# Whole-block stores and head-by-head loads for 18-wide heads, last tokens between projections, paired contraction tails, and new segment orders

## The chip, the cores and the metric

One core of one Trainium2 chip. The metric is device time in microseconds (us), the median of several executions.

Words used throughout: a **segment** is one of 64 turns of a recurrence; a **step** is one unit of ordinary attention (scores of four heads, one exp over 128 x 2048, weighing) that is threaded into the segments. The **loop** is the 64 segments, the **prologue** what comes before the first projection of segment 0, the **end** the last segment and the finish. In the views, a line gives start and length in us, engine, line of the kernel and operation; brackets give the idle time before it and what ended it; `SPq` is a DMA issued by SyncE. `pvv` are the projections of `A`, `psh`, `pss` and `pso` its scores, row sums and weighing, `acc` its output projection, `tm` a copied projection on its way to memory or to `v_sb` (the values). `sb`, `etb` and `ob` are scores, exp and weighing of `B`.

## The reference

```python
g = sigmoid((x * gate_w).sum(-1, keepdims=True))
return g * A(x, mem0, Wq, Wk, Wv, Wo) + (1 - g) * B(B_x, wqkv, wo)

def A(...):                     # x 2048 x 576, 32 heads of 128, 8 memory tokens, segments of 32
    mem = mem0
    for s in range(64):
        h = concatenate([mem, x[32*s:32*s+32]])         # 40 tokens
        q, k, v = h @ Wq, h @ Wk, h @ Wv                # 576 -> 32 x 128 each
        p = softmax(where(mask, q @ k.T * 128**-0.5, -1e9))
        o = (p @ v) @ Wo
        mem, out_s = o[:8], o[8:]                       # the next segment needs mem

def B(...):                     # plain attention, 2048 tokens, 32 heads of 18 = 576/32
    q, k, v = split(B_x @ wqkv); return softmax(q @ k.T * 18**-0.5) @ v @ wo
```

All arrays are bfloat16. `A` is a chain of 64 segments. `B` is 512 steps, and the kernel fills the chain's waits with them.

## The kernel before

A segment's 40 tokens are treated as 32 plus the last 8. The last 8 do not depend on the memory, so their projections are done ahead, for 16 segments at a time ("last tokens"), stored in memory and loaded again. The inner dimension of 576 is four blocks of 128 and a tail of 64 rows; the tail's weights lie in one tile, two halves above each other, and each projection multiplied the tail against all 128 rows, half of them zeros.

```python
def project(x, w, b, k):                     # one of six per segment: Q0 Q1 K0 K1 V0 V1
    pv = bank(k, [P, 512], FP32, "pvv")
    for c in range(NF + 1):                  # four blocks and the tail
        for j in range(4):                   # four column tiles side by side
            rw, cc = w_slice(w, c, ..., 512)
            nc.tensor.matmul(pv[32*j:32*j+32, :], lhsT=ht[:, cc, :], rhs=rw,
                             start=(c == 0), stop=(c == NF), tile_position=(0, 32*j))

def store_v(x, b):                           # V goes to v_sb by four stores for each of V0, V1
    for jj in range(2):
        for u in range(2):
            nc.sync.dma_start(out=v_sb[64*jj:64*jj+CT, ...], in_=sbt[x][64*jj+32*u: ..., :])

def load_kv(g, kc):                          # B's keys, four heads padded to 32 rows each
    kch[g, kc] = bint.tile([P, KC * P], BF16, name="kch", bufs=6)
    loads.dma_start(out=kch[g, kc][:, :], in_=ktd[g, :, kc * KC * P:(kc + 1) * KC * P])
    ...
```

The order in which a segment's instructions are issued is written out by hand as a string. `B` and `E` are the two halves of a step, `Q0` is a projection, `cQ0` its copy out of PSUM, `v0` the four stores of V0, `S0` scores, `x0` exp, `n0` the causal minimum, `p0` row sums, `l0` and `r0` logarithm and inverse, `m0` the division, `w00` weighing, `o00` its copy, `a00` the output projection, `F0` a filler (last tokens of later segments, or output rows). There is one string for segments with seven steps and one for those with eight:

```python
        8: """
        Q0 B E : V0 cQ0 K0 cV0 v0 B / cK0 E : tq0 pq0 Q1 tk0 pk0 cQ1 B / E : S0 K1 tq1 x0 cK1 B n0 tk1 E
        : V1 pk1 pq1 p0 cV1 v1 S1 l0 r0 x1 / B E : F0 m0 n1 w00 o00 F1 cF0 p1 w01 o01 cF1 l1 r1 m1 B F2
        a00 cF2 w10 o10 w11 E : B E : o11 ol a01 a10 h0 a11 g0 B h1 g1 f0 E : f1 ht0 ht1 oh og
        """.split(),
...
LOAD_LAST = "r1"          # where in the last segment the loads for the finish are issued
```

(`:` and `/` let small leftovers of `A` and `B` run.) The number of eight-step segments is whatever is left of the 512 steps: the steps that the prologue has not done. The last-token fillers run out after segment 46; the output rows go on, in two of every four segments.

The softmax here doesn't subtract the row's maximum and nothing guards it: scores larger than these inputs give would overflow.

## Time and profile before

1617.18 us, median of 3 runs (1617.07 to 1620.35); the profiled execution spans 1613.9 us at a mean clock of 0.986. All stage figures are read the same way: the start of the first matmul of the first projection in each segment, in TensorE's timeline.

| stage (profiled run) | before, us |
|---|---|
| prologue | 174.55 |
| segment 0 | 23.02 |
| segments 1 to 22, mean (seven steps) | 21.88 |
| segments 23 to 46, mean | 22.25 |
| segments 47 to 62, mean (eight steps, no last-token fillers) | 21.58 |
| last segment and finish | 55.64 |

First the page's row of the granted clock, in tenths of full speed for 40 slices of the span:

```profile
PEclk9899999999999999999999999999999999999999
```

Then the windows by stage: length, busy time and count of each engine, then the mean granted clock, the DMA share and GB/s. The first line is segments 47 to 62, the second the end:

```profile
1212.97:1558.28 345.31, 315.00 (x5744) 160.33 (x5742) 210.18 (x537) 274.46 (x225) 55.50 (x130) 1.00 0.17 35
1558.28:1613.90 55.62, 44.06 (x571) 28.07 (x571) 33.43 (x77) 31.61 (x46) 11.97 (x23) 0.96 0.49 150
```

And on SyncE's timeline the eight stores of V in one eight-step segment (1320.95 to 1343.00):

```profile
1324.72 11.59 SPq L772 DMA_DIRECT2D v_sb<-tm  x8
```

### The profile page before, as it was taken

The numbers are of one execution on the slowest core, as the hardware profiler recorded it, in microseconds if no ns is written. First come the engines' busy times: TensorE is split into PE (matmuls) and PEld (weight loads), VectorE is DVE, ScalarE is ACT, GpSimd is POOL, SyncE is SP. The second block draws the span as 40 slices with busy tenths as digits, with TensorE's granted clock in tenths as the row PEclk, the third lists the DMA queues.
The fourth block names the chain that finished last, engine by engine and source line by source line (L and its number), as shares of the span: only waits on it lengthen the run. The fifth ranks groups of instructions, "written<-read, shape, count | busy, mean of one in ns | idle before, by whom it ended". The sixth has DMA issues, their size and how long they took to land.

```text
span 1613.9 us, 57766 instructions
## 1 busy us (share of the span) xinstructions
PE 1476.7 (91%) x25082; PEld 782.0 (48%) x25082; DVE 960.0 (59%) x2355; ACT 1139.8 (71%) x981; POOL 338.4 (21%) x731
## 2 busy tenths in 40 slices
PE   6598899999999999999999999999999989998997
PEld 3434444555454444555454445555554444444445
DVE  2233666666566666666566666666666656565656
ACT  2165577777677767777677777777777777788774
POOL 6311211213131031302121211212121212120131
PEclk9899999999999999999999999999999999999999
DMA  7788322212122121212122121212221121211125
GB/s 200 235 291 290 100 65 64 49 42 52 45 50 53 32 53 38 61 36 49 43 43 60 38 50 40 57 39 45 51 53 35 30 48 34 45 34 35 29 59 162
DMA packets 209865, 114.39 MB, mean 71 GB/s; under 512 B 159491, under 2 KB 197251, under 8 KB 208019
## 3 DMA queue, kind: packets, MB, share of 16 engines
q1 hardware_dynamic: 188971, 58.40, 16.1%
q0 software_dynamic: 19696, 50.02, 9.9%
q8 instruction: 196, 3.21, 0.9%
q10 hardware_dynamic: 944, 2.29, 0.4%
q14 instruction: 58, 0.48, 0.1%
HBM read 60.94 MB, written 36.10 MB: 60 GB/s over the span
## 4 chain that ended last, share of the span: by engine, by line
PE 69%; ACT 11%; DVE 11%; DMA 4%; issue 2%; SPq 1%; POOL 1%; DVEq 0%; ACTq 0%; POOLq 0%
PE pvv L755 27%; ACT etb L257 9%; PE sb L238 8%; PE ob L222 7%; PE pt L782 5%; PE pv L326 4%; PE psh L800 3%; PE acc L643 3%; PE pso L838 3%; PE pv L313 2%; DVE hl L657 2%; PE pq L420 2%; DVE hl L654 2%; DVE ot L850 2%; ACT rq L830 2%
## 5 line engine op out<-in xcount | busy, mean ns | idle before, releaser
L257 ACT ACTIVATE etb<-sb 128x2048 bf16<-128x2048 f32 x512 | 959.6, 1874 | 341.9 <-PE sb L238 341.1
L767 DVE CAST tm<-pvv 128x512 bf16<-128x512 f32 x384 | 264.4, 689 | 175.1 <-PE pvv L755 174.2
L755 PEld LDWEIGHTS <-ht 128*32 128x32 bf16 x7680 | 185.8, 97 | 183.7 <-DVE ht L891 14.1
L238 PE MATMUL sb<-qch,kch 32*128 32x512 bf16 x2048 | 203.2, 386 | 38.5 <-ACT etb L257 36.7
L222 PE MATMUL ob<-etb,vch 128*32 128x512 bf16 x2048 | 205.9, 392 | 3.9 <-DVE tq L159 3.9
L850 DVE CAST ot<-pso 128x320 bf16<-128x320 f32 x256 | 120.7, 488 | 104.2 <-PE pso L838 99.9
L643 PE MATMUL acc<-wo,ot 128*32 128x384 bf16 (+1 forms) x4096 | 159.7, 291 | 5.4 <-DVE ot L850 3.3
L755 PE MATMUL pvv<-wq_m,ht 128*32 128x512 bf16 x2048 | 134.2, 382 | 13.0 <-DVE ht L891 8.3
L755 PE MATMUL pvv<-wk_m,ht 128*32 128x512 bf16 x2048 | 134.9, 384 | 0.0
L755 PE MATMUL pvv<-wv_m,ht 128*32 128x512 bf16 x2048 | 134.3, 382 | 0.0
L643 PEld LDWEIGHTS <-ot 128*32 128x32 bf16 x4096 | 105.2, 98 | 46.5 <-DVE ot L850 12.8
L700 POOL DMA_DIRECT2D a_dram<-rl x186 | 92.6, 506 | 162.4 <-DVE rl L695 143.3
L238 PEld LDWEIGHTS <-kch 32*128 32x128 bf16 x2048 | 61.2, 91 | 128.5 <-issue 107.9
L857 POOL COPY otl<-ot 128x256 bf16<-128x256 bf16 x64 | 25.9, 405 | 445.6 <-DVE ot L850 445.6
L222 PEld LDWEIGHTS <-vch 128*32 128x32 bf16 x2048 | 52.9, 93 | 120.6 <-issue 116.0
L782 PE MATMUL pt<-ident,tm 128*128 128x128 bf16 x1024 | 96.8, 221 | 0.8 <-DVE tm L767 0.8
L790 DVE COPY kt<-pt 128x512 bf16<-128x512 bf16 x128 | 54.0, 422 | 69.4 <-PE pt L782 69.0
L838 PE MATMUL pso<-et,v_sb 64*128 64x40 bf16 x2048 | 81.4, 178 | 14.9 <-DVE hll L657 4.7
L838 PEld LDWEIGHTS <-v_sb 64*128 64x128 bf16 x2048 | 62.8, 93 | 62.4 <-issue 49.5
L654 DVE CAST hl<-acc 128x384 bf16<-128x384 f32 (+1 forms) x128 | 57.9, 452 | 58.1 <-PE acc L643 57.8
L782 PEld LDWEIGHTS <-tm 128*128 128x128 bf16 x1024 | 57.8, 98 | 67.0 <-issue 49.4
L826 ACT ACTIVATE lt<-pss 128x320 f32<-128x320 f32 x128 | 56.0, 438 | 43.2 <-PE pss L822 32.8
(141 smaller groups left out, 1847.4 us busy)
## 6 DMA issues: line engine op xcount, KB each, us to landing
v_sb<-tm SPq DMA_DIRECT2D x512, 32.0 KB
wo<-in_A_Wo_dram POOLq DMA_DIRECT2D x4, 1152.0 KB, 9.7
wv_m<-in_A_Wv_dram POOLq DMA_DIRECT2D x4, 1024.0 KB, 8.0
wq_m<-in_A_Wq_dram POOLq DMA_DIRECT2D x4, 1024.0 KB, 9.1
wk_m<-in_A_Wk_dram POOLq DMA_DIRECT2D x4, 1024.0 KB, 8.0
xl<-qld SPq DMA_DIRECT2D x64, 64.0 KB
xl<-kld SPq DMA_DIRECT2D x64, 64.0 KB
v_sb<-vld SPq DMA_DIRECT2D x128, 32.0 KB
```

Of the source, the lines that this page charges most:

```text
L222: nc.tensor.matmul(ob[32 * j:32 * j + 32, :], lhsT=vc[:, o + 32 * j:o + 32 * j + 32], rhs=et4[:, j, :], start=(kb == 0), stop=(kb == NKB - 1),
L238: nc.tensor.matmul(sb[:, j, :], lhsT=kc[32 * j:32 * j + 32, o:o + P], rhs=qch[gq][32 * j:32 * j + 32, :], start=True, stop=True, tile_posi ...
L257: nc.scalar.activation(out=before[:, :, :], in_=sb[:, :, :], func=ACT.Exp, scale=scale_b)
L326: nc.tensor.matmul(pv[:, o:o + P], lhsT=lw, rhs=xlb[:, cc, :], start=(c == 0), stop=(c == NF))
L643: nc.tensor.matmul(acc[32 * j:32 * j + 32, 0:d1 - d0], lhsT=o[:, h, 0:CT], rhs=wo[:, h, d0:d1], start=(b == 0 and i == 0), stop=(b == 1 an ...
L654: nc.vector.tensor_copy(out=hl[:, 0, d0:d1], in_=acc[:, 0:d1 - d0])
L700: eng.dma_start(out=rows4[m, seg - LO:seg, i * n:(i + 1) * n], in_=rl[32 * i + m * LO:32 * i + (m + 1) * LO, :],)
L755: nc.tensor.matmul(pv[32 * j:32 * j + 32, :], lhsT=ht[:, cc, :], rhs=rw, start=(c == 0), stop=(c == NF), tile_position=(0, 32 * j),)
L767: nc.vector.tensor_copy(out=sbt[x][:, :], in_=ps[x][:, :])
L782: nc.tensor.transpose(out=pt[:, which, :, :, :].rearrange("p j (u i) t -> p j u i t", i=4)[:, :, :, i, :], in_=sbt[x][:, i * Dh:(i + 1) * Dh],
L838: nc.tensor.matmul(pso[:, i * L:(i + 1) * L], lhsT=v_sb[64 * jj:64 * jj + 64, b * 1024 + i * Dh:b * 1024 + (i + 1) * Dh], rhs=et[64 * jj:6 ...
L850: nc.vector.tensor_copy(out=ot[:, j * HG:(j + 1) * HG, :].rearrange("p h t -> p (h t)"), in_=ps["o", b, jj][:, 0:W8],)
```

## The change

Four intentions. **Queries and keys of B** are stored in whole 128-row blocks; the padding to 32 rows a head happens at the load, by head, into tiles zeroed once, so nine stores cut at the heads' edges and all pad stores go. **Last tokens** are threaded between the projections of the prologue. **Tails are paired**: two projections' 64-row tails use the upper and the lower half of the array at once. **New orders** for both kinds of segment, as the pairs ask for, made with the projections near the front. The final loads move with the order (`LOAD_LAST`).

```diff
-    qtd = dpool.tile([GB, P, S], BF16, name="qtd")
-    ktd = dpool.tile([GB, P, S], BF16, name="ktd")
+    qkd = dpool.tile([2 * Dm, S], BF16, name="qkd")
...
+        def load_heads(eng, t, f, t0):
+            for j in range(4):
+                eng.dma_start(
+                    out=t[32 * j:32 * j + DhB, :], in_=qkd[f + j * DhB:f + (j + 1) * DhB, t0:t0 + QC]
+                )
...
+    def store_qk(blk):
+        nc.sync.dma_start(out=qkd[blk * P:(blk + 1) * P, :], in_=stgs[blk][:, :])
...
+        for _ in range(2 * min(t, 1)):       # value weights fetched early
+            next(pieces)
...
+    for i, blk in enumerate((1, 6, 2, 7, 3, 8)):
         for t in range(NQC):
             project_qk(blk, t, 0)
             between(1.1)
-        store_qk(blk, range(GB))
+            if i > 0:
+                some_tokens()                # two halves of a last-token block
+        store_qk(blk)
...
+        def project_tails(two):
+            two = [(x, w, b, begin(x)) for x, w, b in two]
+            for j in range(4):
+                for x, w, b, first in two:
+                    t, r = w_tail(w, columns(b, j), 512)
+                    nc.tensor.matmul(
+                        ps[x][32 * j:32 * j + 32, :],
+                        lhsT=ht[TL * r:TL * r + TL, NF + r, :],
+                        rhs=t[TL * r:TL * r + TL, :],
+                        start=first, stop=(not first),
+                        tile_position=(TL * r, 32 * j), skip_group_check=True,
+                    )
...
         8: """
-        Q0 B E : V0 cQ0 K0 cV0 v0 B / cK0 E : tq0 pq0 Q1 tk0 pk0 cQ1 B / E : S0 K1 tq1 x0 cK1 B n0 tk1 E
-        : V1 pk1 pq1 p0 cV1 v1 S1 l0 r0 x1 / B E : F0 m0 n1 w00 o00 F1 cF0 p1 w01 o01 cF1 l1 r1 m1 B F2
-        a00 cF2 w10 o10 w11 E : B E : o11 ol a01 a10 h0 a11 g0 B h1 g1 f0 E : f1 ht0 ht1 oh og
+        Q0 B T0 cQ0 K0 T1 E : cK0 B K1 E : Q1 cQ1 B cK1 V0 T2 E : tk0 tq0 pk0 B E : pq0 / V1 S0 cV0 v0
+        tq1 B cV1 v1 tk1 pq1 x0 F1 n0 pk1 E : p0 / S1 / cF1 x1 n1 l0 F2 F0 p1 r0 l1 r1 m0 cF2 B cF0 w00
+        m1 E : w01 o00 o01 w10 w11 a00 o11 o10 ol B a01 h0 a10 g0 E : a11 h1 B f0 g1 ht0 f1 E : ht1 og
+        oh
...
-    LOAD_LAST = "r1"
+    WIDE = max(ORDERS)
+    LOAD_LAST = [n for n in ORDERS[WIDE] if n[0] in "QKVT"][-1]
```

Left out: the same for the seven-step order, the banks, the four-tile row sums and last-token values, and setup moved forward.

## The prediction

> **What bounds the kernel now.** I read the page first, then TensorE's timeline stage by stage, then SyncE's and ScalarE's timelines for the stages that are not full. From the page:
>
> ```profile
> PE   6598899999999999999999999999999989998997
> ...
> ACT  2165577777677767777677777777777777788774
> ...
> PE 69%; ACT 11%; DVE 11%; DMA 4%; issue 2%; SPq 1%; POOL 1%; DVEq 0%; ACTq 0%; POOLq 0%
> ```
>
> TensorE is full from the fifth slice on, and 69% of the chain of waits is its work. The timeline puts the first recurrent projection (L755) of segment 0 at 174.55 us, of segment 28 at 789.15 and of segment 63 at 1558.28. So there are a prologue of 174.5 us, 28 segments with seven attention steps at 21.95 us each, 35 with eight at 21.97, and 56 us of last segment and finish. One more attention step costs next to nothing; so the eight-step segments are not bound by TensorE's work alone. One of them on TensorE:
>
> ```profile
> 1015.82 1.04 PE L755 MATMUL pvv<-wk_m,ht 128*32 128x512 bf16 x16
> 1016.69 0.39 PE L755 MATMUL pvv<-wk_t,ht 128*32 128x512 bf16 x4
> 1017.01 0.40 PE L238 MATMUL sb<-qch,kch 32*128 32x512 bf16 x4
> 1017.34 0.40 PE L222 MATMUL ob<-etb,vch 128*32 128x512 bf16 x4
> ...
> 1034.13 0.32 PE L879 MATMUL pw<-sel,hl 128*128 128x32 bf16 x6
> 1034.75 0.27 PE L879 MATMUL pw<-sel,hl 128*128 128x32 bf16 x4 [0.31 <-DVE hl L657]
> ```
>
> Starts are read, not durations, because matmuls overlap. Sixteen projection matmuls take 0.87 us from start to next start: four groups of four, 0.217 us a group. From the last group to sb it is 0.32, so 0.10 more, and sb to ob is 0.33; but where ob (128*32) is followed by a projection (128*32) it is 0.23. A change of tile shape costs 0.10 us. ScalarE in the same segment:
>
> ```profile
> 1027.90 0.44 ACT L826 ACTIVATE lt<-pss 128x320 f32<-128x320 f32 x1
> 1028.37 0.47 ACT L830 ACTIVATE rq<-lt 128x320 bf16<-128x320 f32 x1
> 1028.74 1.86 ACT L257 ACTIVATE etb<-sb 128x2048 bf16<-128x2048 f32 x1
> 1031.54 1.88 ACT L257 ACTIVATE etb<-sb 128x2048 bf16<-128x2048 f32 x1 [0.94 <-PE sb L238]
> 1033.97 1.88 ACT L257 ACTIVATE etb<-sb 128x2048 bf16<-128x2048 f32 x1 [0.56 <-PE sb L238]
> ```
>
> sb has one buffer, so exp and sb take turns; 2.43 us is the closest that two exps come. The small activations start 0.35 to 0.47 us apart, and one of them fits into the gap between two exps.
>
> The prologue's holes, on TensorE and then on SyncE:
>
> ```profile
> 24.59 2.03 PE L447 MATMUL pvb<-wb,xT 128*128 128x288 bf16 x10 [4.45 <-DVE stg L291]
> ...
> 78.84 4.73 PE L447 MATMUL pvb<-wb,xT 128*128 128x288 bf16 x20 [15.96 <-DVE xn L291]
> ```
>
> ```profile
> 63.44 2.85 SPq L436 DMA_DIRECT2D qtd<-stg  x8
> 66.34 2.75 SPq L436 DMA_DIRECT2D ktd<-stg  x7
> 69.32 5.61 SPq L455 DMA_DIRECT2D vgd<-xn  x5
> ```
>
> The 16 us hole is a wait for a value buffer, whose store stands on SyncE behind 15 head-by-head stores. The 4.45 us hole is a third stg buffer that the zero tile holds until eight pad stores have landed.
>
> **What the Trainium skill says.** "TensorEngine Tiling (Array Packing)", Key Properties: a change of tiling mode drains the engine, a change of tile does not. The trace agrees: 0.10 us. "TensorE: Matmul & The Clock Gate", Part 3, says that row and column tiling combine, with matmuls of different tiles starting about 4 ns apart. The trace shows it for four row tiles (sb) and four column tiles (pvv) apart, 3 to 4 ns; no run yet shows both at once, which the paired tails need. "DMA: Bandwidth & Descriptors", the section on why a DMA increments its semaphore by 16: a copy uses the largest number of engines up to 16 that divides both outer sizes. By that (an estimate) an 18-row store gets 9 engines and a 128-row one 16. [...]
>
> **The change, part by part.**
>
> *Paired tails.* Now a segment has 6 projections of 5 groups. After, 6 of 4 groups, and 3 steps of 8 matmuls of 64x32, which take one group's time each if eight tiles run together: 27 groups for 30, 3 x 0.217 = 0.65 us less. Each tail step adds a shape change, but the new orders and the row sums (L822, now 128x32) remove others: counted in the instruction order, an ordinary seven-step segment goes from 29 changes to 27, an eight-step one from 34 to 31 or 32, some 0.2 us. So TensorE has 0.7 to 0.85 us less work per segment, 50 us over 64.
>
> How much is seen depends on the exp chain. I followed both new orders with the durations above. In the eight-step order the first four spacings are 2.43 us, for TensorE's work between them was cut to 2.3 to 2.45. Then five small activations come between exp 5 and exp 6: 4.7 us with filler work, 3.8 without. Then 2.7, 2.43, and 2.4 into the next segment: 22.0 us (21.1 in the last 16 segments, without fillers) against 22.3 (21.6) measured now. The seven-step order: four times 2.43, then 4.3, 3.4 and 3.1 over the long TensorE stretches: 20.5, and 20.8 with the odd late DVE copy that now puts 0.5 on the mean.
>
> The loop starts with 24 steps done instead of 29, so 23 segments have seven and 41 eight. Up to the last segment: 23 x 20.8 + 24 x 22.05 + 16 x 21.2 = 1347 us against 1384: **37 less**.
>
> *Whole-block stores, loads by head, no pads.* Nine head-by-head stores and eight pads before the first load become three 128-row stores; the 15 stores ahead of vgd<-xn vanish; the loads become four DMAs of 18 rows in place of one, 24 issues at the start (14 on SyncE at about 0.35 us, so 5 us). The 4.45 hole goes. First stores at 48 us, 1.5 MB landed near 57, loads issued by 62, value stores from 62 instead of 69, landing in 5 instead of 8: the second half of the values ends near 71 instead of 83.4, **12 less**. In the loop GpSimd issues about 200 more DMAs of 0.55 us, 110 us spread over 1400, on an engine that is busy 21%: nothing.
>
> *Last tokens between projections.* After that both kernels have 24 projections and 24 token blocks of 1.1 us, and 24 steps of 0.66 in place of 29: 53 + 16 = 69 us, 71 to 140, plus 4 for late copies and stores. Now it is 83.4 to 174.5, 91 us for 72 of work: TensorE waits for exp where only 1.2 us lie between steps (0.5 each time), 3.9 us for a DVE that itself waits for a token store, about 9 us for qld<-tm in the chain, and 4 for DVE's setup. With 2.2 us of other work per step, weights of the values fetched early and the setup moved forward, these mostly go. Start of the loop near 144: **30 less** in all, of which I take off 2 for the first segment, which gets the output weights late (their fetch can only start when the projections end).
>
> *Final loads.* In the last segment their 28 issues on SyncE (1573.9 to 1588.2, 14.3 us) move ahead of the eight v_sb stores. Weighing needs those some 5 us after V1; they will come at 20 us into the segment instead of about 12. I expect 8 us of wait there, against 2 now: **6 more**.
>
> Sum: -37 - 28 + 6 = -59, set against 1617 and rounded towards the known: **1560 us**, 3.5% less.
>
> **The rivals.**
> *The exp chain takes the gain.* Eight-step segments are at 22 us whatever TensorE does, and the seven-step ones keep waits like those now (1.5 us over their bare work). For: one more step costs nothing today. Against: the new orders visibly lay TensorE's stretches at 2.43. Loop gain 5 to 15 us: 1585.
> *Paired tails don't overlap.* If two row halves of one column strip run one after the other, each tail step is 0.43 and the 0.65 us are lost: 64 x 0.65 = 42 us back, 1595 to 1600. Against: both kinds of tiling are seen to overlap singly. One in ten.
> *The prologue is hidden or bound by transfers.* 14 MB of weights still have to land, and DMA is 0.8 to 0.9 busy from 60 to 160 us now. If the early value weights slow the x tiles, or the output weights hold the first segment, 10 to 15 us of the 28 are lost: 1573.
> *The loop follows TensorE's work fully.* 50 us from work and another 10 from waits: 1540.
>
> **Range and chances.** The prologue is uncertain by about 7 us, the loop by 15, the end by 4. That gives 1540 to 1586 around 1560. The 2% line is 1585; only the first rival with a bad prologue, or the second, cross it. Chances: 0.84 faster, 0.14 same, 0.02 slower.
>
> **What would show each step right or wrong.** In the timeline a tail step should be 8 matmuls with 0.35 us to the next start; 0.55 would mean no overlap. The first L755-like projection should stand near 144 us, with no 16 us hole before the second half of the values. Segments of 20.8, 22.05 and 21.2 us; equal spacing near 22 in all would be the first rival. Exps 2.43 us apart four times in a row. In the last segment, weighing (pso) waits for v_sb, some 8 us in all. The prediction is wrong if tails serialize, if the loop starts after 155, or if eight-step segments stay at 22.3 and seven-step ones above 21.5.

## The result, and the profile after

1666.78 us, median of 4 runs (1664.27 to 1669.87), against 1617.12 us for the kernel before on the same chip: ratio 1.0304, 95% interval 1.0282 to 1.0326. **Slower by 3%**, results correct. The stages of the profiled run, which was the slowest of the four (1669.87 us):

| stage | before | predicted | after | after less predicted |
|---|---|---|---|---|
| prologue | 174.55 | 144 | 154.48 | 10.5 |
| segment 0 | 23.02 | 22.8 | 32.70 | 9.9 |
| segments 1 to 22, mean | 21.88 | 20.8 | 21.27 | 22 x 0.47 = 10.3 |
| segments 23 to 46, mean | 22.25 | 22.05 | 23.31 | 24 x 1.26 = 30.2 |
| segments 47 to 62, mean | 21.58 | 21.2 | 23.91 | 16 x 2.71 = 43.4 |
| last segment and finish | 55.64 | 61.6 | 71.14 | 9.5 |

The last column sums to 114 us, of which the forty eight-step segments have 74. The page of the kernel after, the rows that answer to those shown of before:

```profile
PE   7798899999999999999999999999988889889857
...
ACT  2165577777777776777777777777777777777754
...
PEclk9799899999999999999999999999999898989978
...
PE 54%; ACT 14%; DVE 12%; DMA 8%; SPq 6%; issue 3%; POOL 2%; ACTq 0%; DVEq 0%; POOLq 0%
```

TensorE is busier early (the prologue is shorter), and then has 8s where it had 9s, from the slice where the last-token fillers run out. TensorE's share of the chain of waits fell from 69% to 54%; DMA and SyncE's queue now have 14% together. And the clock row shows 8s. By windows, again segments 47 to 62 and the end:

```profile
1214.45:1597.00 382.55, 337.96 (x5837) 165.35 (x5837) 204.35 (x536) 278.30 (x225) 71.58 (x163) 0.89 0.15 30
1597.00:1668.10 71.10, 45.29 (x580) 27.89 (x577) 33.02 (x77) 31.59 (x46) 11.95 (x23) 0.82 0.39 117
```

The clock, 1.00 before, is 0.89 in the sixteen late segments and 0.82 in the end. The clock records know two values, 1.0 and 0.5. The halved clock covers 116.1 us of the loop (17.1 before), 25.6 of the end (5.0 before) and 27.3 of the prologue (23.9 before).

One eight-step segment (segment 53, 24.1 us long) on TensorE, its second half:

```profile
1364.27 0.41 PE L798 MATMUL pvv<-wv_t,ht 64*32 64x512 bf16 x8
1364.61 0.62 PE L825 MATMUL pt<-ident,tm 128*128 128x128 bf16 x8
...
1369.42 0.32 PE L866 MATMUL pss<-et,bsel 128*32 128x320 bf16 x4 [0.75 <-DVE et L858]
1369.76 0.58 PE L843 MATMUL psh<-qt,kt 128*64 128x40 bf16 x16
1370.86 0.35 PE L702 MATMUL pl<-hll,sel 128*32 128x192 bf16 x6 [0.52 <-ACT et L854]
...
1374.16 0.31 PE L889 MATMUL pso<-et,v_sb 64*128 64x40 bf16 x4 [0.34 <-DMA v_sb<-tm]
1374.41 1.47 PE L662 MATMUL acc<-wo,ot 128*32 128x384 bf16 x16
1375.81 0.61 PE L261 MATMUL sb<-qch,kch 32*128 32x512 bf16 x4
```

The first two lines show that the paired tail is what it was meant to be: eight matmuls of 64 rows by 32 columns, 0.34 us from their start to the next. Below, after the projections have ended, TensorE has small things with waits between them, and at 1374 it is half as fast: sixteen output matmuls take 1.47 us here and 0.83 us where the clock is full, the four score matmuls 0.61 for 0.40. The same segment by windows, split where the clock changes:

```profile
1356.70:1373.00 16.30, 14.43 (x246) 6.74 (x247) 8.10 (x22) 13.38 (x13) 0.28 (x1) 1.00 0.07 20
1373.00:1380.81 7.81, 7.21 (x106) 3.71 (x105) 3.72 (x10) 3.91 (x3) 7.81 (x17) 0.57 0.29 44
```

And SyncE in that segment:

```profile
1367.91 4.96 SPq L815 DMA_DIRECT2D v_sb<-tm  x8
```

The eight stores stand one behind the other, 0.62 us each, with the projections of V done late; weighing starts at 1372.13, and its last four matmuls of 32 wait 0.34 us for them, until 1374.16. In this segment that is little; over the run TensorE waits 42.0 us for these stores, for 4.6 before. (The view counts waits over 150 ns. Counting those from 50 ns on too, as the experiments below do, it is 26.9 in the loop and 16.2 in the last segment.) On ScalarE the exps from the fifth of this segment on:

```profile
1368.12 1.88 ACT L280 ACTIVATE etb<-sb 128x2048 bf16<-128x2048 f32 x1 [0.23 <-PE sb L261]
...
1372.52 1.86 ACT L280 ACTIVATE etb<-sb 128x2048 bf16<-128x2048 f32 x1
1376.48 1.88 ACT L280 ACTIVATE etb<-sb 128x2048 bf16<-128x2048 f32 x1 [2.10 <-PE sb L261]
1380.16 1.88 ACT L280 ACTIVATE etb<-sb 128x2048 bf16<-128x2048 f32 x1 [1.80 <-PE sb L261]
```

They come 4.40, 3.96 and 3.68 us apart, where 3.8, 2.7 and 2.43 were predicted. ScalarE waits up to 2.10 us for the scores here, 0.56 us in the first part of the segment.

In the last segment the loads for the finish stand ahead of the v_sb stores:

```profile
1608.01 2.21 SPq L1050 DMA_DIRECT2D wq_m<-in_B_wo_dram  x5
1610.33 2.08 SPq L1052 DMA_DIRECT2D wq_m<-in_B_wo_dram  x4
1613.27 8.38 SPq L1055 DMA_DIRECT2D wq_m<-otd  x15
1621.70 1.77 SPq L1055 DMA_DIRECT2D wk_m<-otd  x4
1623.57 4.96 SPq L815 DMA_DIRECT2D v_sb<-tm  x8
```

```profile
1626.44 0.64 PE L889 MATMUL pso<-et,v_sb 64*128 64x40 bf16 x12 [13.61 <-DMA v_sb<-tm]
```

The second fence is TensorE: 13.6 us of wait in one place. In segment 0, GpSimd copies the last tokens of queries and keys late:

```profile
153.83 1.81 POOL L581 DMA_DIRECT2D wo<-in_A_Wo_dram  x2 [41.12 <-DMA kld<-tm]
...
166.07 0.88 POOL L581 DMA_DIRECT2D wo<-in_A_Wo_dram  x1 [4.14 <-DMA wo<-in_A_Wo_dram]
...
170.55 0.40 POOL L1112 COPY qt<-xl 128x256 bf16<-128x256 bf16 x1
```

GpSimd can fetch the output weights only when their memory is free, at 153.8; it then stands in its own queue, because the fetches are made to go two at a time; so it is 166 before it gets to other work and 170.6 before it copies. The first scores wait 9.6 us for that.

### The profile page after: what moved, and what is told of

It is laid out like the page before. It is cut to its first block, busy times and chain, and to the rows that moved or that the text cites. A ratio compares the mean times of both kernels' runs of the same rounds, so it can differ in the third digit from the quotient of the medians. Undisturbed runs are those within 1.5% of the kernel's fastest.

```text
span 1668.1 us, 59667 instructions
## 1 busy us (share of the span) xinstructions
PE 1493.2 (90%) x25946; PEld 782.8 (47%) x25946; DVE 940.8 (56%) x2363; ACT 1143.9 (69%) x981; POOL 417.0 (25%) x890
## 4 chain that ended last, share of the span: by engine, by line
PE 54%; ACT 14%; DVE 12%; DMA 8%; SPq 6%; issue 3%; POOL 2%; ACTq 0%; DVEq 0%; POOLq 0%
PE pvv L783 13%; ACT etb L280 13%; PE sb L261 9%; PE acc L662 6%; PE ob L245 6%; DMA v_sb<-tm 5%; SPq L815 4%; PE pt L825 3%; PE pv L355 3%; PE pq L442 3%; PE psh L843 2%; PE pvv L798 2%; DVE ot L901 2%; POOL a_dram L719 2%; DVE hl L676 2%
## 5 line engine op out<-in xcount | busy, mean ns | idle before, releaser
L810 DVE CAST tm<-pvv 128x512 bf16<-128x512 f32 x384 | 256.5, 685 | 249.7 <-PE pvv L783 148.6
L261 PE MATMUL sb<-qch,kch 32*128 32x512 bf16 x2048 | 208.6, 394 | 18.5 <-ACT etb L280 12.0
L783 PEld LDWEIGHTS <-ht 128*32 128x32 bf16 x6144 | 154.9, 96 | 146.7 <-issue 10.6
L662 PE MATMUL acc<-wo,ot 128*32 128x384 bf16 (+1 forms) x4096 | 173.2, 317 | 3.0
L901 DVE CAST ot<-pso 128x320 bf16<-128x320 f32 x256 | 115.4, 484 | 52.2 <-PE pso L889 50.3
L261 PEld LDWEIGHTS <-kch 32*128 32x128 bf16 x2048 | 69.8, 91 | 133.1 <-issue 104.8
L783 PE MATMUL pvv<-wk_m,ht 128*32 128x512 bf16 x2048 | 129.1, 380 | 0.0
L825 PE MATMUL pt<-ident,tm 128*128 128x128 bf16 x1024 | 86.7, 221 | 0.6
L843 PEld LDWEIGHTS <-kt 128*64 128x64 bf16 x2048 | 61.8, 112 | 54.1 <-DVE qt L833 15.3
L843 PE MATMUL psh<-qt,kt 128*64 128x40 bf16 x2048 | 74.8, 189 | 11.3 <-DVE qt L833 10.4
```

The costliest lines, as they stand in the source:

```text
L261: nc.tensor.matmul(sb[:, j, :], lhsT=kc[32 * j:32 * j + 32, o:o + P], rhs=qch[gq][32 * j:32 * j + 32, :], start=True, stop=True, tile_posi ...
L662: nc.tensor.matmul(acc[32 * j:32 * j + 32, 0:d1 - d0], lhsT=o[:, h, 0:CT], rhs=wo[:, h, d0:d1], start=(b == 0 and i == 0), stop=(b == 1 an ...
L783: nc.tensor.matmul(ps[x][32 * j:32 * j + 32, :], lhsT=ht[:, c, :], rhs=w[0][:, c, columns(b, j):columns(b, j) + 512], start=(first and c = ...
L810: nc.vector.tensor_copy(out=sbt[x][:, :], in_=ps[x][:, :])
L825: nc.tensor.transpose(out=pt[:, which, :, :, :].rearrange("p j (u i) t -> p j u i t", i=4)[:, :, :, i, :], in_=sbt[x][:, i * Dh:(i + 1) * Dh],
L843: nc.tensor.matmul(psh[64 * jj:64 * jj + 64, i * L:(i + 1) * L], lhsT=kt[:, h * L:h * L + 64], rhs=qt[:, h, :], start=True, stop=True, til ...
```

## The experiments

Three theories for the forty eight-step segments went into them: **stores** (TensorE waits for v_sb), **clock** (the new order's light stretch halves the clock), and the rival that **paired tails** themselves cost (they do not overlap everywhere, or ask for more shape changes). The other stages had theories of their own. All kernels below are the kernel after with the edit shown, all were correct, and all ratios are to the kernel before on the same chip in the same rounds. "Halved" is the time at half clock in the loop; stage figures are from the profiled runs.

| run | ratio | prologue + segment 0 | 1–22 | 23–46 | 47–62 | end | halved, loop |
|---|---|---|---|---|---|---|---|
| before | 1 | 197.6 | 21.88 | 22.25 | 21.58 | 55.6 | 17.1 |
| after | 1.0304 | 187.2 | 21.27 | 23.31 | 23.91 | 71.1 | 116.1 |
| e1 | 0.9869 | 185.5 | 21.23 | 22.18 | 21.65 | 67.1 | 27.3 |
| e2 | 1.0230 | 185.9 | 21.30 | 23.64 | 23.96 | 57.0 | 133.1 |
| e3 | 1.0296 | 186.2 | 21.24 | 23.20 | 23.97 | 73.1 | 112.6 |
| e4 | 1.0060 | 187.0 | 21.27 | 22.55 | 23.08 | 69.4 | 85.3 |
| e5 | 1.0348 | 186.1 | 21.40 | 23.95 | 23.25 | 70.6 | 13.7 |
| e6 | 1.0319 | 188.1 | 21.25 | 23.92 | 22.99 | 69.9 | 20.5 |
| e7 | 1.0407 | 184.5 | 21.41 | 23.68 | 24.51 | 73.4 | 116.1 |
| e8 | 1.0152 | 188.7 | 21.19 | 22.62 | 23.94 | 67.3 | 112.6 |
| e9 | 0.9979 | 184.4 | 21.27 | 22.55 | 22.10 | 69.6 | 20.5 |
| e10 | 0.9844 | 185.6 | 21.22 | 22.31 | 21.73 | 54.8 | 27.3 |
| e11 | 1.0336 | 185.5 | 21.45 | 23.48 | 23.94 | 69.6 | 136.5 |
| e12 | 1.0330 | 186.6 | 21.54 | 23.33 | 24.01 | 72.4 | 122.9 |
| e13 | 1.0319 | 182.0 | 21.36 | 23.55 | 23.92 | 72.4 | 129.7 |
| e14 | 0.9814 | 184.1 | 21.37 | 22.32 | 21.69 | 55.0 | 30.7 |

### e1: the eight-step segments in their old order

```diff
-        Q0 B T0 cQ0 K0 T1 E : cK0 B K1 E : Q1 ...         # order 8, new
+        Q0 B E : V0 cQ0 K0 cV0 v0 B / cK0 E : tq0 ...     # order 8 of before, and its banks
-        todo = segment(s, BANKS[width])
+        todo = segment(s, BANKS[width], paired=(width == 7))   # own 128-row tails in these
```

> The eight-step segments alone go back to the old order and the old, unpaired projections; all else is as after. My theory (the eight-step order itself is what went wrong: its softmax steps and its v_sb stores lie so close together that TensorE waits, and its clock then drops): segments 23 to 46 come down from 23.3 to about 22.3 us and 47 to 62 from 23.9 to about 21.6, the halved-clock time of the loop from 116 us to about 20, and the whole from 1667 to about 1605. Rival (the loads by head and the pair of stores disturb the loop whatever the order): segments stay above 23 us and the whole above 1650.

Measured 1600.96 us, before 1621.62: 0.9869 (0.9841 to 0.9897). The eight-step segments are back at 22.18 and 21.65, the waits for v_sb in the loop at 5.9 us, the halved clock at 27.3 us. So the whole loss, and more, is in the new eight-step segments (their order, or their paired tails, for the edit takes both away): without them the rest of the change is worth 1.3%. It does not yet tell which part of them.

### e2: the final loads at their old place

```diff
-    LOAD_LAST = [n for n in ORDERS[WIDE] if n[0] in "QKVT"][-1]
+    LOAD_LAST = "r1"
```

> Only the point of the final loads goes back to where it was, after the stores of v_sb. If those 28 DMAs ahead of the v_sb stores cost what the trace shows (13.9 us of wait at the first weighing of the last segment and 3 more after it), the whole is 13 to 16 us shorter, 1652; the stretch from the last segment's start to the end is 56 to 58 us instead of 71. Rival (the finish then waits for its loads instead): less than 5 us.

Measured 1662.25, before 1621.62: 1.023 (1.0189 to 1.0271). The end falls from 71.1 to 57.0 us, 14 us; waits for v_sb there from 16.2 to 1.3. By the ratios the whole is 0.0074 x 1620 = 12 us shorter. The mechanism that the prediction gave for the end is right, its size was not.

### e3: the output weights' fetches without turns

```diff
-        in_turn(
-            nc.gpsimd.dma_start(out=wo[:, 8 * q:8 * q + 8, :], in_=...)
-        )
+        nc.gpsimd.dma_start(out=wo[:, 8 * q:8 * q + 8, :], in_=...)
```

> The four fetches of the output weights no longer wait for each other, so GpSimd is free for the copies that the first scores need. If GpSimd's wait is what makes the first segment 32.7 us, it falls to 24 to 26 and the whole is 6 to 9 us shorter, 1659. Rival (the segment is bound by the landing of the weights themselves): the wait moves on to the output projection, and less than 3 us is gained.

Measured 1671.35: 1.0296 (1.0262 to 1.0331). No gain: segment 0 took 35.1 us. GpSimd was free at 157 us, and then waited 12.95 us for the token tile of the next segment (xg), which stands ahead of the copies. The wait had changed its name only. This theory of segment 0 fell.

### e4: half of the stores on another queue

```diff
                 for u in range(2):
-                    nc.sync.dma_start(
+                    (nc.gpsimd if b else nc.sync).dma_start(
                         out=v_sb[64 * jj:64 * jj + CT, ...
```

> The four v_sb stores of the second projection go to GpSimd's queue, the other four stay on SyncE. The waits of the weighing for v_sb are 42 us in the trace of after, about 17 of them in the last segment. If SyncE's issue of eight stores in a row (5 us) makes them late, the waits in the loop fall from about 25 us to under 5, some halved-clock stretches vanish with them, and the whole is 25 to 40 us shorter, about 1635. If the stores are late because of the projection and its copy, nothing changes (within 5 us).

Measured 1633.94: 1.0060 (1.0026 to 1.0094), so 0.0244 x 1620 = 39 us less than the change. Waits for v_sb in the loop fell from 26.9 to 5.1 us; segments 23 to 46 from 23.31 to 22.55, the late ones from 23.91 to 23.08. The halved clock fell as well, from 116 to 85 us. A wait is a stretch without matmuls, so the two may go together (see the table under e9), but this run does not part them: the 39 us hold 22 us of waits in the loop and whatever the 31 us of halved clock cost. So the store theory is shown, with about half of the loss; 23.08 is still far from 21.65.

### e5 and e6: dummy matmuls in the light stretch, everywhere

```diff
+        def dummies(ps_, n):                 # eight-step segments only, unused columns of the bank
+            for _ in range(n):
+                nc.tensor.matmul(ps_[:, W8:512], lhsT=ident[:, :], rhs=wo[:, 0, 0:512 - W8], ...)
         def sums(b, k):
             ps["p", b] = bank(k, [P, 512], FP32, "pss")
+            dummies(ps["p", b], 8)
...
             pso = bank(k, [P, 512], FP32, "pso")
+            dummies(pso, 4 if b else 0)
```

e5 has these alone, e6 has the edit of e4 too.

> As after, with dummy matmuls (128x128 on 192 columns, eight ahead of each row sum and four ahead of each weighing of the second half, 24 a segment, about 2 us of TensorE work) into unused columns, in the eight-step segments alone, at places where TensorE waits. If the halved clock is a cost of its own, set off by the slack stretch around the row sums, the halved-clock time of the loop falls from 116 us to under 40 and the last 16 segments from 23.9 to 22.5 us, although TensorE has more to do; the whole is about 20 to 30 us shorter than after. If the halved clock only accompanies the waits, the dummies add their own time, up to 1 us a segment, and the whole is 0 to 40 us longer.

> The split v_sb stores and the dummy matmuls together. If waits for v_sb and the halved clock are the two halves of the loss in the eight-step segments, segments 47 to 62 come to about 22 us (23.1 with the split stores alone), those of 23 to 46 stay near 22.5 as fillers keep TensorE busy there, and the whole is near 1620. If the dummies only cost time, it is above 1640.

Measured 1674.0 (1.0348, 1.0325 to 1.0371) and 1669.41 (1.0319, 1.0302 to 1.0335), before 1618.46. The halved clock was gone, 13.7 and 20.5 us, and the time was not better; for e6 1620 had been expected. In segments 47 to 62 e5 gained (23.91 to 23.25), but in 23 to 46, where fillers keep TensorE busy, the dummies only added their own work (23.31 to 23.95). The experiment shows that work raises the clock; it cannot tell what the clock costs, for the cure cost as much. e9 repairs that.

### e7: the new orders without pairing

```diff
-        todo = segment(s, BANKS[width])
+        todo = segment(s, BANKS[width], paired=False)     # each projection takes its own tail
```

> As after, with the same orders, but each projection takes its tail with its own 128-row matmuls again, and the tail steps are empty. My prediction had pairing worth 0.65 us of streams less 0.3 of shape changes a segment. In the seven-step segments, which follow TensorE's work, that is 0.3 to 0.6 us a segment: segments 1 to 22 go from 21.27 to about 21.7. In the eight-step ones it may even out. The whole is 10 to 25 us longer. Rival (pairs do not overlap, so pairing is worth nothing): segments 1 to 22 stay within 0.1 us or get shorter.

Measured 1683.67: 1.0407 (1.0369 to 1.0445), longer than the change. So pairing pays, some 0.010 x 1618 = 17 us, and the rival that it costs is refuted; what e1 takes away is the order. Most of the gain is in the eight-step segments, by the means 0.37 us (23 to 46) and 0.60 us (47 to 62). The seven-step ones gain less than the 0.3 expected here: their median is 21.14 us for 21.02 with pairs, their mean 0.14 more. Of the 0.65 reckoned for the streams, some 0.3 go to three more changes of tile shape (27 for 24 in an ordinary seven-step segment, counted in the traces, at 0.10 us); where the rest goes was not tested.

### e8: the eight-step order made from the seven-step one

```diff
-        Q0 B T0 cQ0 K0 T1 E : cK0 B K1 E : Q1 ...         # order 8, and its banks
+        Q0 T0 B E : cQ0 K1 K0 B Q1 cK0 T1 tq0 ...         # order 7 with one more B E, its banks
```

> The eight-step order is made anew from the seven-step one, with an eighth attention step between the first and the second filler: v_sb stores of the first half go out 2 steps earlier, and the softmax steps are spread. If the eight-step order alone is the loss, by where it puts v_sb stores and softmax, segments 23 to 46 take 21.3 us (23.3 after), segments 47 to 62 about 21 (23.9), the halved-clock time of the loop falls below 20 us, and the whole is 1667 - 48 - 46 = about 1573. Rival (eight steps with paired tails are bound near 22 us by exp and its handover in any order): 22.2 and 21.6 as in the old order, 1605.

Measured 1643.71: 1.0152 (1.0129 to 1.0175). Neither the 1573 us of the expectation nor the 1605 of its rival. Waits for v_sb in the loop are 3.6 us, and segments 23 to 46 take 22.62. But segments 47 to 62 take 23.94, as in the change, and 95.6 of the loop's 112.6 us of halved clock lie in them. With the store waits gone and the clock still halved, the late segments are no better. That fits the clock theory; it does not prove it, for this is another order with waits of its own.

### e9: dummy matmuls only where the fillers have run out

```diff
         fill_bank[0] = k
-        next(later, None)
+        if next(later, "end") == "end":      # nothing left to fill with: eight idle-time matmuls
+            pd = bank(k, [P, 512], FP32, "pd")
+            for _ in range(8):
+                nc.tensor.matmul(pd[:, 0:192], lhsT=ident[:, :], rhs=wo[:, 0, 0:192], ...)
         return lambda: next(later, None)
```

together with the edit of e4.

> The split v_sb stores, and eight dummy matmuls (128x128 on 192 columns, 0.65 us) in each of the two filler places once the fillers have run out, so in twelve of the last sixteen segments alone; there TensorE waits 0.75 and 1.0 us in the trace of after, so the dummies are nearly free. If the halved clock is a cost of its own, set off by a 3.4 us window with little matmul work, the loop's halved-clock time falls from 85 us to under 30, segments 47 to 62 from 23.1 to 22.0 or less, and the whole from 1634 to about 1617. If it only accompanies waits, those segments take 23.1 to 23.7.

Measured 1617.92, before 1622.11: 0.9979 (0.9953 to 1.0005), as expected (segments 47 to 62 take 22.10, just over the 22.0). Against e4 the only difference is work that nobody needs, and it makes the kernel 0.0081 x 1620 = 13 us faster (6 to 20 by the two intervals, for the two ran on different chips). The windows of segments 47 to 62, first e4, then e9:

```profile
1196.09:1565.30 369.21, 335.29 (x5838) 164.58 (x5838) 204.59 (x537) 277.99 (x225) 103.40 (x227) 0.91 0.16 31
```

```profile
1193.39:1547.03 353.64, 329.06 (x6028) 172.72 (x6028) 204.08 (x537) 278.07 (x225) 103.77 (x227) 1.00 0.17 32
```

190 matmuls more, clock 1.00 for 0.91, TensorE's busy time less by 6 us though it does more, and the stretch shorter by 15.6 us. That is the clock's cost there, less what the dummies cost.

What makes the clock fall can be read from the traces of nine runs (before, after, e1, e4, e5, e8, e9, e10, e14). The clock records change on a grid of 3.413 us. For each such window in segments 1 to 62 I added up the matmuls that start in it, each as its columns at 2.4 a nanosecond (the trace's 0.217 us for 512 columns is within 2% of that) times the share of the array that its tile covers, and divided by 3.413 us. That is the window's occupancy. Of windows at full clock,

| occupancy of the window | windows | next window at half clock |
|---|---|---|
| below 0.30 | 45 | 45 |
| 0.30 to 0.40 | 45 | 23 |
| above 0.40 | 3431 | 1 |

All sixteen runs counted in the same way give 146 of 146, 45 of 95 and 1 of some 5970. The weighting by the tile's share matters: without it, 67 of the 69 windows that a halved one follows lie above 0.40. So in these windows small tiles counted for little, however tightly they stood in time.

In segment 53 above, the windows from 1362.7 on have 0.81, 0.45, 0.28, and then the clock is halved for 6.8 us. The longest single wait of TensorE in segments 1 to 62 of the kernel after is 2.16 us, so no window was empty. The table is a correlation, and its bounds hold for this kernel's mix of tiles; that work in the window changes the clock, and with it the time, is what e9 shows.

### e10: the best of the parts

The edits of e1, e2 and e3, with the copies of the last tokens ahead of the next segment's token tile.

> What the runs so far say is worth keeping: the new prologue and the paired seven-step segments; the old order for eight steps, final loads after the v_sb stores, output weights without turns and the copies for the first scores ahead of the next segment's. From 1601 with the old eight-step order: 14 less at the end, 0 to 7 less in the first segment: 1580 to 1588, that is 2% under before. If the parts hinder each other, above 1595.

Measured 1596.04: 0.9844 (0.9817 to 0.9871). It beats both kernels, but it is slower than the 1580 to 1588 expected and at the mark set for parts that hinder each other (1595): the end gave its 12 us (54.8 for 67.1 in e1), segment 0 nothing (33.3 for 32.5).

### e11 and e12: what holds segment 0 and the prologue

e11 is e3's edit, and the copies go first:

```diff
-        if s + 1 < n_seg:
-            put_x(s + 1)                     # waits for the next segment's tokens
         for jj in range(2):
             nc.sync.dma_start(out=v_sb[64 * jj + CT:64 * jj + L, :], ...)
         for dst in (qt, kt3):
             nc.gpsimd.tensor_copy(out=dst[:, :, CT:L], in_=xls.pop(0)[:, :, :])
+        if s + 1 < n_seg:
+            put_x(s + 1)
```

e12 takes the early fetch of the value weights away:

```diff
-        for _ in range(2 * min(t, 1)):
-            next(pieces)
```

> As after, output weights without turns and GpSimd's copies for the scores ahead of the copy of the next segment's tokens. The run without turns showed that this copy then waited 12.9 us for its own load behind the output weights. If the order on GpSimd is what is left, the first segment falls from 32.7 to 25 to 27 us and the whole is 6 us shorter. If the loads of the last tokens are themselves late behind 4.7 MB of weights, it stays above 31.

> As after, without the six early fetches of the value weights. If those crowd out the x tiles (the 3.9 us wait for xn at 42 us) and with it bring on a halved clock at 52 us, the first scores come at about 75 us instead of 82.9 and the loop starts at 147 instead of 154.5, unless a later weight comes late. Rival (the stores, the loads by head and the mem0 load set the time): within 2 us of 82.9.

e11: 1675.65 (1.0336, 1.0308 to 1.0364). Segment 0 took 35.6 us, no shorter. On GpSimd:

```profile
149.43 3.56 POOL L580 DMA_DIRECT2D wo<-in_A_Wo_dram  x4 [39.75 <-DMA kld<-tm]
...
169.64 0.40 POOL L1107 COPY qt<-xl 128x256 bf16<-128x256 bf16 x1 [13.44 <-DMA xl<-qld]
```

The wait is now for the small load of last tokens itself (64 KB), issued on SyncE at 150.74, among the four fetches of 1.15 MB, and landed only at 169.6, just as the last of these lands (169.4).

e12: 1674.5 (1.033, 1.0301 to 1.0359). The first attention scores came 5 us earlier, at 77.9 us, but the loop began at 155.2 instead of the 147 expected: TensorE waited 3.14 us for the weights at 87.6, and the projections took 77 us in place of 71.6. With the early weights the first scores come 5 us later; without them the time is paid later.

### e13 and e14: the output weights behind the small loads

```diff
-    for q in range(4):                       # in the prologue
-        in_turn(nc.gpsimd.dma_start(out=wo[:, 8 * q:8 * q + 8, :], in_=...))
...
         for dst in (qt, kt3):
             nc.gpsimd.tensor_copy(out=dst[:, :, CT:L], in_=xls.pop(0)[:, :, :])
+        if s + 1 < n_seg:
+            put_x(s + 1)
+        for q in range(4 if s == 0 else 0):
+            nc.gpsimd.dma_start(out=wo[:, 8 * q:8 * q + 8, :], in_=...)
```

e14 has this on the version of e10.

> The changed kernel, but the four fetches of the output weights are issued in the first segment, after GpSimd has copied the last tokens of queries and keys. If the fetches hold the two small loads back (my theory), the last tokens' keys land near 154 us instead of 169, the first scores follow some 15 us earlier, and the output projection then waits some 4 us for the weights: loop start plus first segment near 178 us instead of 187, whole kernel some 7 us shorter, about 1660. If the small loads are late for their own reason (their stores, or the queue they stand in), the first segment stays near 33 us and the kernel at 1667 or, with the weights later still, longer. Halved clock in the loop stays at 115 to 135 us in both.

> The same late fetch on the best version (old order and unpaired projections in the eight-step segments, final loads at their old place). Theory: 7 us off 1596, so 1589, 0.98 of the kernel before. Rival: 1596 or more.

GpSimd in e13:

```profile
155.57 0.40 POOL L1103 COPY qt<-xl 128x256 bf16<-128x256 bf16 x1 [0.18 <-DMA xl<-qld]
157.41 0.40 POOL L1103 COPY kt<-xl 128x256 bf16<-128x256 bf16 x1 [1.44 <-DMA xl<-kld]
```

Issued at 152.8, the load has landed by 155.6: under 3 us, where among the fetches it took 19. That settles what held the small loads. Prologue and segment 0 came down from 187.2 to 182.0 us, not to the 178 expected, because weighing then waited 3.3 us for v_sb, the clock was halved after it, and the output projection waited 1.5 us for the weights. The whole of e13 was 1672.24 (1.0319, 1.0301 to 1.0338), not the 1660 expected: its loop had 30.3 us of waits for v_sb and 129.7 us of halved clock, more than the change itself, which may hide the 5 us. e14 is 1590.49 us, before 1620.7: 0.9814 (0.9795 to 0.9833), against 0.9844 (0.9817 to 0.9871) for e10. The intervals overlap, and in the profiled runs prologue and segment 0 differ by 1.5 us only (184.1 for 185.6), so a gain of the late fetch in the whole time is not shown. **e14 has the lowest time**, 1.9% under the kernel before; e10 is not to be told from it.

## Why the prediction was wrong

It said 1560 us and faster; it is 1667 and slower. By its own steps:

**Paired tails overlap: right.** 0.34 us a tail step for 0.35 predicted (what no run had shown at the time, row and column tiles at once, is seen here), and unpaired is slower (e7). The rival at one in ten is refuted. The saving is mis-sized: the working set the new tail steps against fewer shape changes elsewhere and left 0.7 to 0.85 us a segment, but pairing itself is worth 0.12 to 0.14 us in a seven-step segment and 0.37 to 0.60 in an eight-step one (e7).

**Seven-step segments of 20.8 us: right in kind, a little short.** The sixth spacing of the exps is 3.99 us on the mean for 3.4 reckoned, the others near the sum. The median of segments 1 to 22 is 21.02 us, from 21.57; the mean 21.27 has single waits for v_sb of up to 1.75 us in it. 10 us of the miss.

**Eight-step segments of 22.05 and 21.2 us: this is the step that failed.** "I followed both new orders with the durations above" counted the order's matmuls and small activations at full clock and let every operand be there in time. The spacings of the exps, on the mean in the trace of after, show where it broke:

| spacing, us | 1st to 4th | 5th | 6th | 7th | 8th |
|---|---|---|---|---|---|
| predicted, with fillers | 2.43 | 4.7 | 2.7 | 2.43 | 2.4 |
| segments 23 to 46 | 2.43 to 2.44 | 5.41 | 3.13 | 2.59 | 2.44 |
| predicted, without | 2.43 | 3.8 | 2.7 | 2.43 | 2.4 |
| segments 47 to 62 | 2.43 to 2.45 | 4.85 | 4.00 | 2.86 | 2.44 |

The first four are as predicted. The failed terms are the fifth to the seventh, where softmax, weighing and output projection lie: 1.3 us too short with fillers, 2.8 without. What was not in the sum: (1) the new order puts V1's projection late and the eight v_sb stores in one row, 4.96 us of issue and their landing, in front of weighing. e4 takes that away: 39 us of the whole, some of it through the clock. (2) It gathers the heavy projections in front and leaves a light stretch behind, and light windows are followed by halved clock: 81.9 of the 382.6 us of segments 47 to 62. e9 takes that away (3.4 us left): another 13 us. From e9 (0.9979) to e1 (0.9869) 18 us are left, which lie in the other waits of that order, such as 0.75 us for the causal minimum in the segment shown, and in the dummies; these I did not pull apart. The prediction listed equal segments near 22 (the exp chain) as the first rival. It is not refuted: no run with the new orders brought the eight-step segments under what the old one takes (22.18 and 21.65 in e1), so whether paired tails can gain there in any order stays open. What happened in them was in none of the rivals: more than the gain was lost, to two things that no engine's work shows. The kernel before had both almost at zero (4.6 us and 17.1 us), and so its profile did not show them; the new order's text would have had to be read for where work is thin and where stores queue.

**The prologue at 144 us: half right.** The two holes went, and from the first scores to the loop it was 71.6 us for the 71 reckoned. But the first scores came at 82.9 us and not near 73. The second half of the values did end at 73.0 (71 reckoned); the failed term is the value stores, "from 62 instead of 69, landing in 5": the first of them was issued at 67.6 us, behind the loads by head (61.1 to 67.5 on SyncE, held until DVE had zeroed their tiles at 61.1), and one whose buffer a copy of the last values needs took 10.0 us to land (70.05 to 80.02). The hole behind these stores became smaller and moved; it did not vanish. Before the first scores TensorE waits in small pieces, for token tiles (3.92 us), the memory tokens (3.10) and a copy (4.24), and the clock is 0.68 and 0.75 on the mean from 41 to 62 and from 62 to 82.9 us. The third rival, that transfers bind, named this and sized it too small: prologue and segment 0 lost 20 us of the 28, not 10 to 15. The early weights cost the first scores 5 us, though taking them away did not bring the loop forward (e12). How many DMA engines an 18-row store gets, which the prediction estimated, no run here shows.

**Segment 0 plus 2 us: right cause, wrong size.** The late fetch of the output weights did hold it, by 9.9 us more, and through the small loads behind it (e3, e11 and e13), not through the weights themselves.

**Final loads plus 6: right cause, too small.** 8 us of wait were expected; one wait was 13.6, all for v_sb in the end 16.2 us. e2 gives 14 us back.

**GpSimd's extra issues in the loop cost nothing: right.** Its busy time rose from 338 to 417 us, giving it still more (e4) made the kernel faster, and e1, which has these issues too, ran the old eight-step order as fast as before (22.18 and 21.65 for 22.25 and 21.58).

## What to carry to other kernels

A new order of the same work is not priced by its longest engine alone: look for where it gathers the stores (a queue that takes 0.6 us for each, just ahead of their reader) and where it thins TensorE's work out, for there the clock halved (here after every window of 3.4 us with less than 0.30 of the array's work). Compare the clock row of both profiles before anything else; if it falls in a stretch that nothing fills, useless matmuls in idle slots are a quick test, and a better order the cure. And here a large fetch that was issued together with small loads held them until it was through (19 us for under 3); issue the small ones first, even when the large one is wanted soon.

## What the Trainium skill lacked or had wrong

- "TensorE: Matmul & The Clock Gate", Part 1: it gives the two clock states, the 3413 ns window and, under "HAM oscillation — how this bites in real kernels", a rule about idle gaps over about 3.4 us. The states and the window agree with these traces. The rule is too weak as a guard: no wait in segments 1 to 62 of the kernel after was over 2.16 us, and the clock was halved for 102 us of them. "A second HAM failure mode" on the same page does speak of micro-idles, without a number. These runs give one: below 0.30 occupancy of a window (matmul columns weighted by the tile's share of the array) 45 of 45 were followed by half clock, from 0.30 to 0.40 23 of 45, above 0.40 1 of 3431.
- The same page's Terms put the penalty of throttled time at half of it. Here 61.5 us less of halved clock in segments 47 to 62 (64.9 in e4, 3.4 in e9) made that stretch 15.6 us shorter, a quarter. Half was too much here; how far TensorE's other waits and the dummies' own time make up the difference was not tested.
- I found on no page how long stores or loads queue at their issuing engine when a row of them is ready at once: eight 32 KB stores took 4.96 us on SyncE (0.62 us each), 28 loads 15.6 us (1608.01 to 1623.57).
- Nor a figure for what large fetches do to small loads issued among them: a 64 KB load took 19 us among four of 1.15 MB, and under 3 us ahead of them.
